# A new written-out issue order for a fused S4 convolution and Hedgehog attention kernel

## The chip, the cores and the metric

The kernel runs on one core of one Trainium2 chip. The metric is device time in microseconds (us), the median of several runs. Shorter is better.

## The reference

For tokens u of shape 1 x 2048 x 512 the kernel computes a gated mix of two branches:

```python
g = sigmoid((u * gate_w).sum(-1, keepdims=True))
# branch a: S4 convolution, one kernel of length 2048 per channel
K = real(einsum("dn,dnl,dn->dl", C, exp(dt * A * l), dt * B))   # 512 channels, 128 states
a = irfft(rfft(pad(u)) * rfft(pad(K)))[:2048] + u * Dskip
# branch b: linear attention, 32 heads of 16, with a learned feature map
q, k, v = split(u @ wqkv)                      # both branches read u
phi(t) = concat(softmax(t @ w_phi), softmax(-(t @ w_phi)))
o = (phi(q) @ (phi(k).T @ v)) / (phi(q) @ phi(k).sum(0) + 1e-6)
b = o @ wo
return g * a + (1 - g) * b
```

## The kernel before, in words

The kernel is not written as loops that run in order. Five builder functions (`prepare`, `keys_and_spectrum`, `attention_keys`, `plan_queries`, `plan_conv`) add 1046 nodes to a `Plan`. A node is one step on one engine: a group of matmuls on TensorE (PE), one or a few instructions on VectorE (DVE) or ScalarE (ACT), or the issue of DMAs from SyncE (SP). Nodes are created unit by unit, but `Plan.run` calls them in the order that the string `ORDER` gives: two characters for each node, a number in base 64. Each engine runs its own instructions strictly in the order in which they were issued, and the framework adds the semaphores that the data needs. So `ORDER` decides what stands in front of what in each of the four queues. Four more strings go with it:

- `SIDES`: for each node that may run on either of two engines, which one. These are mostly the copies out of PSUM (ACT or DVE), and some output DMAs (SP or ACT).
- `RINGS`: for each PSUM tile that may lie in either of two rings (`ps`, and `p0` early or `pf` late; two buffers each), which one.
- `FOURS`: for each of 16 units of 32 channels, whether the two partial products of the tile `A` are added on DVE (`A3`, line 1077) ahead of 64 matmuls, or left apart, with 128 matmuls.
- `ZPS`: for each of 8 pairs of token tiles, whether PE sums the exponentials of the keys in groups of four (`zp`, line 697) ahead of a short DVE reduction (line 706), or DVE reduces them alone (two instructions, line 703).

A node is named here by its kind and its number in the order of creation. What the names mean, in the order of the stages:

- Start: `par`, `wtr`, `xtr`, `ud`, `wv`, `wsm`, `ld` load parameters and tokens (`wtr` and `xtr` transpose on the way). `tg1`, `tgs`, `tga` build Fourier tables. `st1` to `st3`, `pzw` and `pzr` split the state matrix and carry it through DRAM. `psri`, `p_t`, `p_d`, `p_px` and others starting with `p_` build polar tables. `wps` and `wpe` fold `w_phi` into the weights, and `at1` lays `w_phi` out for that.
- Keys: `pk` (PE), `ek` (ACT, two exponentials), `zk` (DVE), `rz` (ACT), `vp` (PE), `vb` (a copy), `vr` (DVE), `kn` (PE). `gps` is the gate's product.
- Spectrum of u, between the keys: `udc`, `psAu`, `XAu`, `psBu`, `XU`, and `xuw`, which stores the tile `xst` to DRAM as `XUd`. `xst` has two buffers.
- Kernel generation for 16 units: `argC` and `cs` (sines), `argE`, `E` and `El` (exponentials), `A1`, `A2`, `A3`, `Rh`, `Rl` (DVE products), `kps` (PE), `KD` (a copy). ACT switches its table between sines and exponentials (`tabT`, `tabL`).
- Transforms for quarters of the channels: `psA`, `XA`, `psB`, `XK`, `t128`, `t64` or `t32` (DVE), `psz`, `Zr`; `zw` stores Z to DRAM, `zr` reads it back turned; `psy` (PE) and `ou` (DVE, with the gate). The last unit goes through `pszn`, `Zn` and `psyn` without DRAM.
- Queries: `pq`, `eq`, `zs`, `z1` to `z5`, `aw`, `ar`, `em`, `ops`, `oT`, `pya` or `bps`, `bs3`, `bsg`. Names that end in L belong to the last of the four blocks of queries. `out` and `outL` store the result.

SP issues all loads and nearly all stores, in one queue.

Of the kernel before, what the change touches and what calls it, by code (L numbers as in the profile page):

```python
# [70 lines left out]
class Plan:  # L71

    DIGITS = "0123456789abcdefghijklmnopqrstuvwxyzABCDEFGHIJKLMNOPQRSTUVWXYZ-_"
    ORDER = ("0B0C000a0H0K012K0L0j0k0I0J0l2E0D0g0d0y0M0P0_0S2F0z070U0V042H0T052I2B112J2x0E0A2z0s0p0q140m12020W0Y0N0X0n0v2y0b0e0h0i0O0Z"
             "100Q0616080f0t1d13150u2C192L2M171a1b0-"
             "1c0R1n1o1p1e1y1H031q1w0c181f1g1I2G091x1S1z1A1J1r1R1O1B0F0G2R2S1s2T2U1E1C1Q2N1K2P2D2Q2O4r1F1Y4q4x4z4E4F4y4A4M4N4B4C4I4J1M"
             "1N4D4K4G4O4T4P0r0w0x4X1Z4U4Q4R4S4Y4H4L4s4_51504V4W522v56571P4Z0o2V5a53544-2W5b555e5f2X1h582Y5c5g5l5h2Z2_5p1D2-"
             "3159305d5i5j335m5q5k325t5v5u5w1i1G34355n5r37381T365A5o5s5x5B393b1j3c5y5E5I5F5K5z1t3a3d3f5C5G5P5J3F3e3k5D3g3h3m5L3l3n1U5T"
             "5M5N3r5H5Q5O2w3t3u6a6c1u1V5U5R3G5V3o3s3H3I4t5S3y5W5X6b3A3B6d5Z3z3C6e1W5Y5-3J1L3K6f6g5_60613L3N3v3M3O3P3Q3w2A1X1-"
             "3R3T27201_213p223i3S1k283V1l3U292d622a233W3X3Y3Z2b2e3-"  # L80
             "243_1m402c2f252o2g2h4144453x46472q262i4b3D482p4d2j4c2k496h2l3E4e4i2r4k4l2s4a2m2t2n421v4f4v4j3j2u8a4m4n3q4w6i89636j646667"
             "43688e6l8d65694g4o8b6m6n8f4h4p888c6k6o8k8l6p6t718h8g8_6q8m8q8i906u8j8n8o6v6w6x8r8w8N6y6z6A8p8s8x8t6B8u8O6C728E6D6E8F737A"
             "7B758v8y746F927C8K768G6G6H8z8L777D8A8C8P6I6r78798B8H8I8Tab8J8U8Dac6J7a7ba27E7F91a38M7c8Q7G7H7d9U7e8R9Y9Z8S8V8W6K6L6M6N6P"
             "6Qa49V9-6O6T6Vad6Ra56Sa87f9Xa07g7Ia9a69W9_7h7i6s6Ua18X8Y93ahapaq7J7j8Za76X6Zaiar7K8-ay9baz7k7l6-"
             "7L7M7maa9caebL7N6YbPaf986W9d7q7r7n7o7pavag7sbQajakaA949j9kaw7u7ObMbR9l7v7P7Qasat7w9eaE9f9r9z95969sbOau7R9A7SbT7T7U9galam"
             "aF6_anaoax7xbNaB7Z7t7ybS7-"
             "bUbVbWaPaCaD97aG9t7VaMaN7zaH999aaQ9B9m9n4uaO7W7X9oaI7YaKaSaJaL7_bY9u80bX81bZ9v9wb_aYaZ8384c09CaR9Dc2c38270aT8586a-"
             "aU879EaVa_b0b1aW9x9ycgchb-"
             "9p9qc1c4c8c9c5b49hc6bcb5b6bdcicmc7cnbe9i9F9GdMdNdOdPcp9HcacbbkbldQdRb7b8cqcDcjckdScGb2dTcldUdV9I9J9N9O9P9KcvaXbfbgb9cc9L"
             "9McecrcfdW9QcocHbmcwcscdctezeAbh9RcE9SeIeJeBdCcudDdXdYdG9TdIeKdHcxcybabncFczcJdZcBcAcCeCeDeFe1e2eGbocPcQcRd-"  # L90
             "cXd3dFcYeEeHd4cIbpeOcZcSc-endKbbeoepd_e0e3dbeLcTdEcKcMcUc_d0e4d1cVcLdJbqdLbibjbrb3bsdcbtbyePeMeNfRcNd5fSd2bueQeRcOddbvd6"
             "d7bwd8fXdedffoeSetbzfrfsbAfpfubxeUeVfqe5fvfTdgeubBeTbCbDd9e6evdhcWeWeqerf2f3esdpeXftfwfxdidaeYf4eZfyfYfUfVbEfzdjdkdldqdm"
             "dndre-fWf5f6fAdsfBewe_exf7f8f0fCdodte7f9bIeyfDf1fZfafdfefffEduf-f_dvg0fbg1fFfce9fGg2e8eddzeefHg3g4g5eaebg6fgbJfIg7g8dwfh"
             "g9gagbfJfMfNbFfifKbGgcecfOefegeheiejfLflgdgebKgffPfQekfjdAelfmfndxdyggfkghdBemgjgkglgibH")
# [532 lines left out]
def attention_keys(P, nc, g, psum, r):  # L627
# [40 lines left out]
    for s2 in range(8):  # L668
# [20 lines left out]

        def ps4(K=K, box=box, on=P.ZPS[s2] == "1"):  # L690
            if not on:
                return
            box.ps = bank("zk")
            for u in range(2):
                e = K.E[:, u].rearrange("p g (h a b) -> p (g h) a b", a=4, b=4)
                for k in range(4):
                    nc.tensor.matmul(box.ps[:, 256 * u:256 * u + 256], lhsT=g.ident[:], rhs=e[:, :, k, :], start=(k == 0), stop=(k == 3), skip_group_check=True)

        def rd(K=K, box=box, on=P.ZPS[s2] == "1"):
            K.Z = g.kwk.tile([128, 2, 2, 32], F32, name="Zk")  # L700
            if not on:
                for u in range(2):
                    nc.vector.tensor_reduce(out=K.Z[:, u].rearrange("p g h -> p (g h)"), in_=K.E[:, u].rearrange("p g (h f) -> p (g h) f", f=16),
                                            axis=mybir.AxisListType.X, op=ALU.add)
                return
            nc.vector.tensor_reduce(out=K.Z[:].rearrange("p u g h -> p (u g h)"), in_=box.ps[:].rearrange("p (z b) -> p z b", b=4), axis=mybir.AxisListType.X, op=ALU.add)
            box.ps = None
# [318 lines left out]

def plan_conv(P, nc, g, psum, r):
# [566 lines left out]
```

## Time and profile before

| what | value |
|---|---|
| median of 3 runs | 261.48 us (260.12 to 264.59) |
| span of the profiled execution | 263.8 us, 9862 instructions |
| busy: PE | 199.3 us, 76% |
| busy: DVE | 225.5 us, 85%, 306 instructions |
| busy: ACT | 215.2 us, 82%, 300 instructions |
| busy: POOL | 10.2 us, 4% |
| DMA | 38.0 MB, mean 144 GB/s |

The span is the time from the first to the last instruction of the profiled execution; the page gives no other time for it, so this is taken as its own time. It lies 2.3 us above the median of the runs. More than three quarters of the chain that ended last lies on DVE (37%), PE (20%) and ACT (20%): no one engine holds it all along, and the stages must be read one by one.

### The profile page before, as it was taken

How to read it: one execution, taken by the hardware profiler on the slowest of the kernel's cores; microseconds unless marked ns; L12 is line 12 of the kernel's file. 1: busy time of each engine (PE TensorE's matmuls, PEld its weight loads, DVE VectorE, ACT ScalarE, POOL GpSimd, SP SyncE). 2: the span in 40 equal slices, each digit the busy share in tenths (PEclk: the TensorE clock that was granted, in tenths of full speed). 3: DMA queues.
4: the chain of work that ended last, by engine and by line, in shares of the span. 5: the costliest groups of instructions: out<-in, count | busy, mean ns of one | idle time of the engine just before them, and what ended most of it. 6: DMA issues, size and time to landing. Idle time of an engine off the chain costs nothing.

```text
span 263.8 us, 9862 instructions
## 1 busy us (share of the span) xinstructions
PE 199.3 (76%) x4394; PEld 137.6 (52%) x4416; DVE 225.5 (85%) x306; ACT 215.2 (82%) x300; POOL 10.2 (4%) x22
## 2 busy tenths in 40 slices
PE   0028999999856557898776869789997699989850
PEld 0018445755544323464454648555875667965640
DVE  5579396998799999999999998999999999996330
ACT  4947489995999998999999998999969999573230
POOL 4018000000000000000000000000000000000000
PEclk9999999999997799999886897999999999999995
DMA  7989991006181683602317154267656369897676
GB/s 172 148 165 232 183 204 39 4 2 210 34 252 29 192 244 93 194 4 80 107 53 187 46 187 142 82 202 200 195 150 210 102 211 233 244 227 145 128 132 102
DMA packets 79627, 38.01 MB, mean 144 GB/s; under 512 B 58593, under 2 KB 74593, under 8 KB 79585
## 3 DMA queue, kind: packets, MB, share of 16 engines
q1 hardware_dynamic: 77440, 36.66, 55.2%
q10 hardware_dynamic: 2144, 0.72, 1.3%
q8 instruction: 34, 0.56, 1.0%
q14 instruction: 9, 0.07, 0.1%
HBM read 21.12 MB, written 13.11 MB: 130 GB/s over the span
## 4 chain that ended last, share of the span: by engine, by line
DVE 37%; PE 20%; ACT 20%; issue 9%; DMA 9%; SPq 1%; POOL 1%; ACTq 0%; DVEq 0%; POOLq 0%
DVE R L1088 4%; DVE A L1072 4%; PE pk L676 4%; DVE R L1084 3%; PE vp L724 3%; DVE A L1067 3%; DVE E L1020 2%; DVE t L1198 2%; DMA XUd<-xst 2%; ACT L65 2%; DMA ZT<-Zd 2%; ACT Ek L68 2%; ACT cs L68 2%; DVE Eq L880 2%; ACT XK L147 2%
## 5 line engine op out<-in xcount | busy, mean ns | idle before, releaser
L68 ACT ACTIVATE cs<-args 128x1024 bf16<-128x1024 f32 x32 | 30.9, 1068 | 0.8 <-PE args L990 0.8
L181 PE MATMUL kps<-R,A 128*32 128x64 bf16 x1536 | 28.6, 232 | 2.7 <-DVE A L1072 1.4
L181 PEld LDWEIGHTS <-A 128*32 128x32 bf16 x1536 | 26.4, 161 | 7.0 <-DVE A L1072 2.0
L1067 DVE TENSOR_TENSOR A<-Ctab,Dtab 128x2048 bf16<-128x2048 bf16 x16 | 19.5, 1220 | 0.7 <-PE kps L181 0.7
L68 ACT ACTIVATE Ek<-pk 128x512 bf16<-128x512 f32 x32 | 16.8, 604 | 3.8 <-PE pk L676 3.8
L1088 DVE TENSOR_TENSOR R<-E,cs 128x2048 bf16<-128x2048 bf16 x16 | 19.5, 1221 | 0.1
L1084 DVE TENSOR_TENSOR R<-E,cs 128x2048 bf16<-128x2048 bf16 x16 | 19.5, 1221 | 0.0
L1072 DVE TENSOR_TENSOR A<-Ctab,Dtab 128x2048 bf16<-128x2048 bf16 x16 | 19.5, 1220 | 0.0
L147 ACT CAST XK<-psB 128x1024 bf16<-128x1024 f32 (+1 forms) x17 | 16.2, 994 | 2.4 <-PE psB L194 2.0
L68 ACT ACTIVATE E<-args 128x1024 bf16<-128x1024 f32 x16 | 16.9, 1060 | 1.0 <-PE args L1012 1.0
L724 PE MATMUL vp<-WW,xT 128*128 128x512 bf16 x59 | 16.7, 411 | 1.1 <-issue 0.9
L1198 DVE TENSOR_TENSOR t<-XUX,XK 128x2048 bf16<-128x2048 bf16 x14 | 16.9, 1222 | 0.2 <-ACT XK L147 0.2
L68 ACT ACTIVATE Eq<-pq 128x512 bf16<-128x512 f32 (+1 forms) x28 | 16.7, 696 | 0.2 <-PE pq L810 0.2
L676 PE MATMUL pk<-WW,xT 128*128 128x512 bf16 x58 | 16.2, 410 | 0.7 <-issue 0.5
L147 ACT CAST XA<-psA 128x1024 bf16<-128x1024 f32 (+1 forms) x15 | 14.6, 1015 | 2.5 <-PE psA L188 2.4
L147 ACT CAST Zr<-psz 128x1024 bf16<-128x1024 f32 x15 | 15.4, 1043 | 0.9 <-ACT Zr L147 0.6
L810 PE MATMUL pq<-xT,Wqp 128*128 128x512 bf16 x64 | 15.3, 380 | 0.6 <-ACT Eq L68 0.6
L1230 PE MATMUL psz<-t,TI 128*128 128x512 bf16 x49 | 14.6, 381 | 0.9 <-ACT E L68 0.3
L583 PE MATMUL psB<-XAu,TB 64*128 64x128 bf16 x256 | 10.3, 226 | 6.2 <-ACT xst L147 4.8
L147 ACT CAST xst<-psB 128x1024 bf16<-128x1024 f32 x12 | 11.8, 1040 | 2.8 <-DMA XUd<-xst 2.7
L65 ACT ACT_TABLE_LOAD x10 | 12.8, 1283 | 0.9 <-PEq L1578 0.7
L194 PE MATMUL psB<-XA,TB 128*128 128x128 bf16 (+2 forms) x192 | 10.3, 204 | 4.0 <-ACT XA L147 2.2
(201 smaller groups left out, 477.3 us busy)
## 6 DMA issues: line engine op xcount, KB each, us to landing
XUX<-XUd SPq DMA_DIRECT2D x32, 256.0 KB
XUd<-xst SPq DMA_DIRECT2D x8, 512.0 KB
ax<-apd SPq DMA_DIRECT2D x16, 256.0 KB
Zd<-Zr SPq DMA_DIRECT2D x15, 256.0 KB
ZT<-Zd SPq DMA_DIRECT2D x12, 256.0 KB
UD<-in_A_u_dram SPq DMA_DIRECT2D x16, 128.0 KB
XUd<-xst SPq DMA_DIRECT2D x8, 256.0 KB
out_dram<-xT SPq DMA_DIRECT2D x6, 96.0 KB
```

Of the source, the lines that this page charges most:

```text
L65: return self.nc.scalar.preload_act_table_set(name)
L68: return self.nc.scalar.activation(**kw)
L147: self.nc.scalar.copy(out=o, in_=i)
L181: nc.tensor.matmul(kps[32 * dj:32 * dj + 32, g4, e, :], lhsT=A[:, ka, :, :, d].rearrange("p a b -> p (a b)"), rhs=R[:, kr, d, :], start=(i ...
L676: nc.tensor.matmul(box.ps[:], lhsT=xT[:, st, kt, :], rhs=g.WW[:, kt, :], start=(kt == 0), stop=(kt == 3))
L724: nc.tensor.matmul(box.ps[:], lhsT=xT[:, st, kt, :], rhs=g.WW[:, 4 + kt, :], start=(kt == 0), stop=(kt == 3))
L810: nc.tensor.matmul(box.ps[:, m - m0, :] if late else box.ps[:], lhsT=g.Wqp[:, kt, 128 * m:128 * m + 128], rhs=xT[:, 4 * b:4 * b + 4, kt, : ...
L1067: nc.vector.tensor_tensor(out=c.A[:, 0:2].rearrange("p o a b c -> p (o a) b c"), in0=g.C[U // 8][:, 0:2, :, d0 % 256:d0 % 256 + 32].rearra ...
L1072: nc.vector.tensor_tensor(out=c.A[:, 2:4].rearrange("p o a b c -> p (o a) b c"), in0=g.C[U // 8][:, 1:3, :, d0 % 256:d0 % 256 + 32].rearra ...
L1084: nc.vector.tensor_tensor(out=c.R[:, :, :, 32:64], in0=t.E[:, 1].unsqueeze(1).to_broadcast([128, 2, 32, 32]), in1=t.cs[:], op=ALU.mult)
L1088: nc.vector.tensor_tensor(out=c.R[:, :, :, 0:32], in0=t.E[:, 0].unsqueeze(1).to_broadcast([128, 2, 32, 32]), in1=t.cs[:, ::-1, :, ::-1], o ...
L1198: nc.vector.tensor_tensor(out=box.t, in0=Ls[r0 // ns].X[:], in1=box.XK[:].unsqueeze(1).to_broadcast([128, 2, 1024]), op=ALU.mult)
```

## The change

The five strings are replaced; nothing else. The operations are the same but for what `FOURS` and `ZPS` select. The diff, with the long strings cut:

```diff
-    ORDER = ("0B0C000a0H0K012K0L0j0k0I0J0l2E0D0g0d0y0M0P0_0S2F0z070U0V042H0T052I2B112J2x0E0A2z0s0p0q140m12020W0Y0N0X0n0v2y0b0e0h0i0O0Z"
...
+    ORDER = ("0H0I0J0L0g0h0i190K0M2x0S0y0z0A0W2y000T0P0X0N0U0405060_0708090B0C0D110Y0V0j0k0l2R1216100O0102030d0e0f132B2C2D2N0Z140-0Q17"
...
-    SIDES = ("111110001100000110100100101100000111010000000000111111000011010100000001000010000001000000000100000000000000001000100000"
-             "00000000011000000100000000000000101000101")
+    SIDES = ("101100000000001001000101110101001100000000000000001011101110111111000001110010000001000000000100010000000000001000000000"
+             "00000100001111110000000000000010000011100")
-    RINGS = ("11010000000000000000000000000000000000000000001001000000000000101110110100011101001101110111001001011111110000000")
+    RINGS = ("00111100000000000000000000101000000000000000100100011010000000111100111110100110010111001111110011110100001001011")
...
-    FOURS = ("0101010101011100")
-    ZPS = ("01100011")
+    WARM = ("0")
+    FOURS = ("0111111111111100")
+    ZPS = ("00000110")
```

`WARM`, which asks for matmuls that only keep PE busy, is all zeros before and after.

Read node by node, `SIDES` moves 46 nodes: 26 from ACT to DVE, 17 from DVE to ACT, `at1` from POOL to DVE, and the output DMAs `out#7` and `outL#1` from ACT to SP. To DVE go, among others, three `oT`, all four `bsg`, both `Zn`, `XK#16`, `Zr#14` and `KD#3`; to ACT go six `XAu`, four `vb` (with `vb#0` and `vb#1`), `KD#5`, `KD#9`, `XA#16` and `oTL#1`. `RINGS` moves 43 tiles. `FOURS` adds units 2, 4, 6, 8 and 10 to those without `A3`. `ZPS` turns the PE sum off for pairs 1, 2 and 7 and on for pair 5.

The order itself is read best as the four queues. The first work on the keys, before and after:

```text
PE  before  psri#2 psri#0 psri#1 wps#2 wps#3 wps#0 wps#1 gps#0 pk#0 pk#1 vp#0 pk#2 zp#0 vp#1 pk#3
PE  after   wps#2 wps#0 psri#0 psri#2 wps#3 psri#1 wps#1 pk#0 pk#1 pk#2 pk#3 vp#0 zp#0 zp#1 vp#1 gps#0
DVE before  dt2 w1 st1#1 st2#1 st3#1 st1#0 st2#0 st3#0 p_t#8 p_t#0 p_t#1 p_t#9 p_t#2 p_t#5 p_t#3 wpe#0 p_t#6 p_fc#0 vb#0 zk#0 vb#1
DVE after   w1 dt2 st1#1 st2#1 st1#0 st3#1 p_t#8 p_t#0 p_t#1 st2#0 st3#0 p_t#3 p_t#9 p_t#5 p_t#2 p_t#6 p_fc#0 p_t#4 p_t#7 zk#0 zk#1 vr#0
ACT before  dtc p_e p_g p_d#7 p_d#4 wpe#2 wpe#3 p_d#6 p_d#0 wpe#1 ek#0 ek#1 ek#2 p_d#2 p_d#3 rz#0
ACT after   dtc wpe#2 p_e wpe#3 wpe#0 p_g p_d#7 p_d#2 wpe#1 p_d#0 p_d#3 ek#0 ek#1 ek#2 ek#3 p_d#1 rz#0 vb#0 vb#1
SP  before  wtr par#3 par#0 xtr#3 ld xtr#1 par#5 par#4 wsm par#2 par#1 xtr#2 xtr#0 wv ud#2 ud#1 ud#0 ud#3 pzw#1
SP  after   par#5 wsm par#1 par#2 wtr ld par#0 par#4 xtr#0 par#3 xtr#2 xtr#3 xtr#1 pzw#1 wv ud#0 ud#1 ud#2 ud#3
```

And the last stage:

```text
PE  before  psz#10 psz#11 argE#14 psA#12 psy128#2 psA#13 opsL#0 pya#3 psy128#3 psB64#0 psB64#1 pya#4 kps#14 psz#12 psA#14 psy128#4
            psz#13 psB32#0 pya#5 psy128#5 opsL#1 kps#15 psz#14 psA#15 bpsL#0 bpsL#1 psB32#1 psy64 pszn#0 pszn#1 psyn#0 psyn#1 psy32
PE  after   psz#10 psA#12 psz#11 psA#13 pya#3 psy128#3 argE#15 psB64#0 opsL#0 psB64#1 opsL#1 kps#14 psz#12 psA#14 psz#13 pya#4
            psy128#4 psB32#0 pya#5 psy128#5 kps#15 psz#14 psA#15 bpsL#0 bpsL#1 psB32#1 psy64 pszn#0 pszn#1 psyn#0 psyn#1 psy32
DVE before  t128#11 Rh#15 A1#14 A2#14 ou#2 Rh#14 El#14 Rl#14 El#15 ou#3 A3#14 t64#0 t64#1 Rl#15 A1#15 A2#15 ou#4 A3#15 t32#0 t32#1
            ou#5 KD#9 XA#16 oTL#1 bs3#3 t32#2 t32#3 ou#6 Zn#1 ou#8 ou#9 ou#7
DVE after   t128#11 A1#14 Rh#14 El#14 A2#14 ou#3 Rl#14 A3#14 t64#0 t64#1 Rh#15 El#15 A1#15 Rl#15 A2#15 A3#15 t32#0 t32#1
            ou#5 Y#2 Zr#14 ou#4 bs3#3 bsg#0 bsg#1 bs3#4 bsg#2 bsg#3 t32#2 XK#16 t32#3 ou#6 Zn#0 Zn#1 ou#9 ou#8 ou#7
ACT before  tabL#4 XK#11 E#15 KD#6 Zr#10 Zr#11 E#14 XA#13 XA#12 oTL#0 XK#13 XK#12 KD#7 Y#1 XA#14 Zr#12 Zr#13 XK#14 out#1 KD#8
            Y#2 XA#15 Zr#14 bs3#4 XK#15 XK#16 bsg#0 Zn#0 bsg#1 bsg#2 bsg#3 outL#1 out#7
ACT after   tabL#4 KD#6 E#14 Zr#10 Zr#11 XA#12 XA#13 E#15 XK#12 Y#1 XK#13 oTL#0 KD#7 Zr#12 XA#14 Zr#13 oTL#1 XK#14 out#1 KD#8
            KD#9 XA#15 XA#16 XK#15
SP  before  zw#10 xup#14 zw#11 xup#13 zr#4 zr#5 xup#15 zw#12 zw#13 zr#6 zr#7 zw#14 out#3 out#2 zr#8 zr#9 out#0 out#4 outL#0 out#5 out#6
SP  after   zw#10 zw#11 out#0 zr#4 xup#14 zr#5 zw#12 zw#13 zr#6 zr#7 zw#14 out#3 out#2 outL#1 zr#8 zr#9 outL#0 out#4 out#5 out#6 out#7
```

More of the change, by code (lines that the diff above doesn't have):

```diff
@@ L73 @@
     DIGITS = "0123456789abcdefghijklmnopqrstuvwxyzABCDEFGHIJKLMNOPQRSTUVWXYZ-_"
-    ORDER = ("0B0C000a0H0K012K0L0j0k0I0J0l2E0D0g0d0y0M0P0_0S2F0z070U0V042H0T052I2B112J2x0E0A2z0s0p0q140m12020W0Y0N0X0n0v2y0b0e0h0i0O0Z"
[L75 to L94, printed above, removed]
@@ L95 @@
-    SIDES = ("111110001100000110100100101100000111010000000000111111000011010100000001000010000001000000000100000000000000001000100000"
-             "00000000011000000100000000000000101000101")
-    RINGS = ("11010000000000000000000000000000000000000000001001000000000000101110110100011101001101110111001001011111110000000")
-    WARM = ("000000000000000000000000000000000000000000000000000000000000000000000000000000000000000000000000000000000000000000000000"
-            "000000000000000000000")
@@ L100 @@
-    FOURS = ("0101010101011100")
-    ZPS = ("01100011")
+    ORDER = ("0H0I0J0L0g0h0i190K0M2x0S0y0z0A0W2y000T0P0X0N0U0405060_0708090B0C0D110Y0V0j0k0l2R1216100O0102030d0e0f132B2C2D2N0Z140-0Q17"
+             "151a1b2S0R1w1c1n1H0a0b0c1o1e1d1p1y2H2I2J1I2T2U1z1x2A1A2K2L2M1f1g2E2F2G2O1S1C1J1E1R182P1M1B2Q1F1q1r1s0E0F0G0m0n0o4q1K4x4z"
+             "1N4y4A4M1Y4N4O4E4B0p0q0r1D1G4P4Q4C4R1L4D4F0s0t0u4I4G4J4r4T0v0w0x4K1Z4X4U2V1O4H4s4S4Y2W1T4L4_4V514t2X564Z4W502Y4-521U2Z5e"
+             "532-5a572_54315b1V325f5g5558305c5h5l333459355d5t1P375i5m365j385u5v5k5p5q2v5n395A1h1i1j3b5r5w5o3a5B5s5I3c5x5y5K3d3f5J3F5E"
+             "3g3e5z5C5P5F5L3k3m5M5Q5G3G5D1Q1k1l1m3l3h3i3j5T5H6a5N5O5U6c3H3r3n5R5V5S3o3p3q5W6b6d3I6e1W5X3s5Z3t5Y5-6f3y3u5_3z3A3J606g3B"
+             "1t1u1v611X623K3v3w3x3L3N1-1_3O3P3M2763203R21286h3Q293S2264232b3T3V2d2a3U243W3X3Y3Z3_2f3C3D3E6i252h2c2e403-44462o2j66652g"
+             "456j414243474b2q2i6l2p2l2k262s48494a2w4c4d2r4i4e2m4f4g4h4j2n2t4k2u6m8a674l4m4n4o4v4w89686n4p698e8b6k8d8f6o886p6u8c6w8g8h"
+             "8k8q6t8l8i6y8m8n8j8o6x6v8r6z8w8s716A8p6B8N738O726C8t8x6D8u758E6E8F8G6q6r6s766F8v778P6G8K8y8H788T8I6H7A8L6I6J6K7C748z796L"
+             "6M6N7B8A7a8J8B7b8U6O8C7E8Dab7G7D8M929394ac8Q6P6Q6R7ca27Fa37H7d6T8R6V8_90918S6Sad9U8V7e9Y6X6W6U7f7g7h9Z8W9X6Ya5a87i7j7k8X"
+             "a08Ya49V9-a68Za97Iah9W7lai8-a7aa7q9_a1ayaz7sae7Jap4u6Zaq9b7m7n7oaf7K7r7t7Lag7paj7M9c6-7N7u9jakaMaNaO7O7P7QarbL9d9k7vaEav"
+             "2z9l7w9eas7R7S7T7xbP7U9f6_9rbQ9z9saw9A959697alanat7V7W7X7Z9g9h9iaA7YamaobMaF7_au98999abRaxbO8070bT817-7yaB82aC9t83bN7zaD"
+             "9B84aPaQaRaGbSaHbVbUbYbW85aI869mb_87bXaK9uaJ9nbZc2aSaTaUc0aLcpc39o9p9qc49vaY9Cb4aZcqb-c1c8a-c99w9x9ybcb5cgc59DcGcHcI9E9F"
+             "9Gchb6dMbdc6cicrdNc7dOcmcaaVaWaXdPbecnbkcba_bldQb09H9I9J9K9L9Mcvb7ccb1b2b3dRcjcddSckb8dT9NdUcecfbfbm9OcldVeIeJcwcJcKcLb9"
+             "babbbgcodWdXdYcDcEcFez9PdCbhbibj9QcscteA9RdGdHcueKbnbocxcydZd-d_9SeB9TeFeCdDczdIe1e2e3e0e4cBdEbycCcAdJcPcXeDeGdFeEeOcQcY"
+             "cRdKeHbpbqbrcScZd3bsbtbubvbwbxcTbzd4eLePc-cMcNcOeMdbewexeyd5cUcVcWc_dceNd0d1d2bAeQfoeneoepdddLd6eRfreSfpdeeUd7dfeTeqeres"
+             "bBbCfueVfqd8d9dafRfseWbDe5fvfSeXf2fte7dgdhdibEbFbGbHf3eYe6djdkdlfwf4eZfXfTfxfye-f5fUfzf6e8eteuevfYdpdmdndodqfAfVdsfWdte_"
+             "f0f1f7f8f9fBbIbJbKfCfZfafbfcfDf-f_dudvfEg0e9fdfeffg1fFdreafGfHfIg2dzdAdBedebeceeefdwdxdyg3egg4g6g5g7fgg8ekelemfJfKfLg9fh"
+             "gagbfMfNfOgceheiejgegffifjfkgdflfmfnfPfQggghgigjgkgl")
```

## The prediction

> **What bounds the kernel now.** I read five views: the slices of the page, the table of busy time by stretch, the waits, the groups by line, and the chain that ended last. Instructions carry the names of the plan, numbered from 0 (`zk#1` is the second key sum).
>
> The slices say where to look:
>
> ```profile
> PE   0028999999856557898776869789997699989850
> ...
> DVE  5579396998799999999999998999999999996330
> ACT  4947489995999998999999998999969999573230
> ...
> PEclk9999999999997799999886897999999999999995
> ```
>
> VectorE (DVE) and ScalarE (ACT) are both full from about 30 to 217 us; each is open before 33 us and after 240. The table by stretch gives the idle time (columns: stretch, length, busy time of each engine, clock, DMA share, GB/s):
>
> ```profile
> 0.00:30.00 30.00, 10.68 (x126) 8.55 (x128) 19.45 (x52) 18.67 (x27) 10.19 (x22) 1.00 0.97 181
> 30.00:60.00 30.00, 29.58 (x435) 16.89 (x436) 24.95 (x35) 26.62 (x50) 0.00 (x0) 1.00 0.36 72
> 60.00:75.00 15.00, 12.36 (x264) 8.53 (x260) 11.96 (x16) 12.16 (x25) 0.00 (x0) 1.00 0.51 151
> ...
> 130.00:150.00 20.00, 15.01 (x412) 11.07 (x414) 19.96 (x23) 19.90 (x26) 0.00 (x0) 0.74 0.31 88
> ...
> 217.00:240.00 23.00, 21.88 (x613) 17.64 (x618) 22.05 (x24) 16.02 (x20) 0.00 (x0) 1.00 0.92 226
> 240.00:264.00 24.00, 12.66 (x466) 8.54 (x464) 7.19 (x11) 5.84 (x11) 0.00 (x0) 0.85 0.67 118
> ```
>
> DVE idles 10.6 us before 30, 8.1 from 30 to 75, 3.1 from 75 to 240 (span by span, 165 us less busy time) and 16.8 after. So a new order can gain at the start, between 30 and 75, and at the end; between 75 and 240 it must take work off DVE and ACT together, since both are full. The waits name the three places:
>
> ```profile
> DVE vb L149 <- PE vp L724: 6.4, 3, 4.5
> ...
> DVE t L1201 <- ACT XK L147: 3.5, 1, 3.5
> ...
> ACT xst L147 <- DMA XUd<-xst: 2.7, 1, 2.7
> ```
>
> The sum is made against the profiled execution: span 263.8 us, which is 2.3 above the median of 261.48 and inside the runs' 260.12 to 264.59. I carry the difference over to the median.
>
> **The start: -2.5 us.** Before, TensorE (PE) runs the gate product `gps` (1.9 us) ahead of `pk#0`, and DVE's first key work is `vb#0`, which waits 4.5 us for `vp#0`; `zk#0` starts at 32.67. Now `pk#0` to `pk#3` come first, `gps` later, and `vb#0`, `vb#1` are read by ACT. The last token transpose is issued behind the same other loads, so xT lands as before, at 24.5 (the last count of its semaphore in the trace). The second gate is DVE's polar products, which free PSUM: from `dt2` at 15.9, four instructions of the split (0.6, 0.35, 0.6, 0.6 apart), eight products at 0.6, `st2#0` 0.35 and `st3#0` 1.4 end with `p_t#6` near 24.7, against 26.8. The third, ACT's four copies `wpe`, ends near 22.4 (15.6 + 4 x 1.0 + 0.6 + 1.1 + 2 x 0.55). So `pk#0` starts at 24.8, not 27.3: -2.5. Four matmuls cost 1.7 there (0.42 each in this row, 0.26 later) and `ek` 1.2, so `zk#0` starts between 28 and 30. Bounds: 0 (something else gates) to -4. `at1` moves from POOL to DVE; its nearest DVE row, a 128x1024 product, is 0.69, POOL took 1.50, and it lies under ACT's sines (DVE waits 4.0 us for those). It costs nothing; without that cover, 0.7.
>
> **30 to 75 us: -1.5.** Here PE is 29.58 of 30 busy. ZPS takes the PE pre-sum (1.08) off pairs 1, 2 and 7 and gives one to pair 5: PE -2.2, DVE 3 x 1.74 - 1.74 = +3.5 (L703 below, twice 1.21, against one L706). The 2.7 us of ACT and 1.0 of DVE at 66 are reads of `psB` into `xst`, which has two buffers; the first store takes 5.4 us. Before, 5.4 us of DVE work stands between `XU#1` and `XU#4`; now 7.8 (four at 0.6, `zk#5` now 0.6 to 0.7 by its row if PE is in time, copies, and reads): at least the ACT wait should shrink. `psAu#0` now comes earlier and needs all of UD, which lands about 1.3 us later behind `pzw#1`: 0 to +1 us. Bounds for the stretch: -4 to +2; I take -1.5, nearer to nothing, as the order is tight in new places.
>
> **75 to 240 us: -2.7.** Group rows:
>
> ```profile
> L1077 DVE TENSOR_TENSOR A<-A 128x2048 bf16<-128x2048 bf16 x8 | 9.8, 1220 | 0.0
> ...
> L703 DVE TENSOR_REDUCE Zk<-Ek 128x64 f32<-128x1024 bf16 x8 | 9.4, 1213 | 0.0
> ...
> L706 DVE TENSOR_REDUCE Zk<-zk 128x128 f32<-128x512 f32 x4 | 2.7, 686 | 0.8 <-PE zk L697 0.8
> ```
>
> FOURS drops `A3` (L1077) for units 2, 4, 6, 8, 10: 5 x 1.22 = -6.1 on DVE; each such `kps` has 128 matmuls, not 64: 2.35 against 1.22, 5 x 1.13 = +5.7 on PE, which has room in 108:190 and little after. Up to `A3#15` the reads that leave DVE sum to 14.1 us and `ou#4` (1.22) is put later; those that come, with `at1`, sum to 15.0. With ZPS: -6.1 + 3.5 - 14.1 - 1.2 + 15.0 = -2.9 on DVE. By running sums up to `t128#11` it is -0.8, and -1.3 with the 0.09 us that each of five more back-to-back instructions overlaps. ACT up to the table load `tabL#4` has the same work (-0.3); `E#15` (1.0) now stands behind `Zr#11`.
>
> What this does to the last chain is seen at its head:
>
> ```profile
> 222.94 4.64 DMA Zd<-Zr
> 228.06 4.91 DMA ZT<-Zd
> ...
> 242.44 1.14 DVE oT L149
> 243.63 1.04 PE bps L913 x4
> ```
>
> `Zr#11` goes to DRAM, comes back (9.6 us), and `psy128#4` waits for it; then `pya#5`, `psy128#5`, `opsL#1`, `kps#15` (ends 239.4). Walked with the rows' durations from `t128#11`, taken at 214.1 (219.4 less 4.0 from above and 1.3 of work): `Zr#11` 216.9, `zr#4` 222.3 (5.4 later, as before), `psy128#4` not before 226.7. PE itself reaches it at 227.8 (`kps#14` ends 222.9, then `psz#12`, `psA#14`, `psz#13`, `pya#4`: 1.0, 0.64, 1.0, 2.4). Then 0.63, 0.95, 1.5, 0.63 and `kps#15` 1.21: 232.7. That is 6.7 before 239.4, 4.0 of it from the first two terms: -2.7 is left. Bounds: -0.3 (ACT's saving alone) to -4.6 (DVE's with `kps#15` no longer behind `opsL#1`). In SP's queue `out#0` now stands between `zw#11` and `zr#4` and waits for `ou#3`, at 219.3 in this walk, so it has 3 us to spare; if that cover is gone, each us of `ou#3` is one of `zr#4`. `xup#14` ahead of `zr#5` waits for `t64#0` (222.7) and adds 0.9, covered by `pya#5`.
>
> **The end: -1.1.** Before, `bpsL#1` waits for `oT` on DVE (row above) and `psB32#1` starts at 245.64 behind it; now ACT reads `oT` early: -0.2. All `bsg` and `XK#16` are on DVE in line with `t32#2`, `t32#3`: +0.5. `outL#1` (on SP now, behind `bsg#3`) stands ahead of `zr#8`, `zr#9`: they land up to 1.6 later, `psy32#0` +1.1 at most. After the last product at 257.2 SP still issued this:
>
> ```profile
> 257.13 1.96 SPq L962 DMA_DIRECT2D out_dram<-xT  x2
> 259.13 2.11 SPq L1348 DMA_DIRECT2D out_dram<-xT  x4
> ```
>
> 4.1 us; now only `out#6`, `out#7` are left, four issues, 2.0 us: -2.1. Between -0.9 and -1.5; -1.1. The Trainium skill (DMA: Bandwidth & Descriptors, section Issuing engines are not separate DMA queues) says that issuing from a second engine saves only that engine's issue time; by it the move of `outL#1` and `out#7` from ACT to SP costs 1.0 us each of SP time and nothing in transfer, which is the sum above.
>
> **New waits: +1.5.** A written-out order runs each queue strictly; a late instruction holds all behind it. DVE idles 3.1 us in 75:240 of the order before. I allow half of that; bounds 0 to 8 (the 8.1 of 30:75 once more).
>
> Sum: -2.5 - 1.5 - 2.7 - 1.1 + 1.5 = -6.3: span 257.5, and 261.48 - 6.3 = 255.2; I say 255.
>
> **Rivals.** (1) New waits eat the middle: the reads of PSUM moved (26 to DVE, 17 to ACT, 43 other rings) stop one of the two full queues for 5.7 us, so that only start and end are kept: -2.5 - 1.1 = -3.6, 257.9; with one more us of wait 259. For it: from 108 to 150 both are 99% busy, and no slack absorbs a miss. Against: in running sums of the rows the hand-over from ACT to DVE that is latest against its reader, `E#9` to `El#9`, lags 2.8 us less in the new lists. Chance 0.27. (2) All idle of 30:75 goes and nothing new comes: -2.5 - 4 - 2.7 - 1.5 = -10.7: 250.8. Chance 0.15. (3) Slower: PE becomes the bound from 170 on. It is 63.6 us busy of those 70 (21.88 of 23 at the end) and gets 2 x 1.13 more: 65.9 at full clock. With 4 us of earlier start and 1.5 at the end, PE may take 75.5 before all gain is lost. The granted clock halves in windows of 3.4 us (four between 130 and 161, mean 0.74 in 130:150); one such window loses 1.7 us of matmul, so it decides from six windows after 170; with ten, 65.9 + 17 - 75.5 = +7.4: 269. Against: the clock there was 1.00. Chance 0.10. The Trainium skill (TensorE: Matmul & The Clock Gate, section Part 1: The HAM clock gate) puts the half rate down to an idle window of about 3.4 us; the longest PE gap between 100 and 170 is 1.3 us, so by that rule the halved windows here should not be, and the trace disagrees. (4) The new order does not change the bound: the two full engines take as long as before: 261.5. Chance 0.08. The forecast has 0.40.
>
> **How the numbers follow.** A measurement of this kernel tells about 2% from no change: 256.25 to 266.7. Faster: the forecast's own range, 252 to 258, lies four fifths below 256.25 (0.32); with (2), 0.15, and a quarter of (1), 0.07, that is 0.54. Slower: (3), 0.10, and 0.01 of others. Same: the rest, 0.35. Range for 8 in 10: 249.5 (below (2), by its full bounds) to 262.5 (past (1) and (4)); (3) lies outside.
>
> **What would show it.** Right: `pk#0` near 25, `zk#0` before 30.5; no ACT wait on the XUd store above 1 us; `L1077` x3; DVE idle from 75 to 240 under 5 us; `kps#15` ending 232 to 236; after the last DVE product at most four output DMAs on SP. Wrong: `psy128#4` waiting for ZT behind `out#0`; a PSUM read on DVE or ACT that starts over 1 us late with PE waiting for its buffer; a clock under 0.9 from 170 to 240; `udc#3` waiting for UD.

## The result, and the profile after

| | median | range, runs | ratio to before, 95% interval |
|---|---|---|---|
| before | 262.42 us | 260.12 to 264.59, 4 | |
| after | 270.21 us | 269.06 to 271.32, 4 | 1.0323 [1.0249, 1.0397] |

The new order is 3.2% slower, about 8.5 us (7.8 by the two medians), where 6.3 us of gain was forecast. The profiled execution of after took 269.06 us with a span of 267.0: 2.1 lie around the span. The forecast took the span of before, 263.8, as that execution's own time. A second profile of the same kernel (below) took 263.75 us with a span of 262.0, so the first ran near 265.6, above all four timed runs. The sum compares stages, so it does not move by this, but start stages read from that profile may be late (see the second look below).

Ratios below are to the kernel before on the same chip. They leave out runs more than 1.5% above the fastest of their kernel; where the median of all runs says something else, both are given. A ratio is turned into us with 262.

The slices and the table by stretch of after (the same columns as for before, with 75 to 240 in one row) come first; the last row is before over the same 165 us:

```profile
PE   0241999999855858899758868789998687999760
...
DVE  7687598999999988997799978999989599799841
ACT  6966499998999999999887997899879968884000
...
PEclk9996599999995797999788999999999999999995
```

```profile
0.00:30.00 30.00, 8.65 (x63) 6.24 (x65) 21.03 (x55) 21.10 (x29) 9.81 (x21) 0.87 0.91 167
30.00:60.00 30.00, 29.63 (x493) 17.51 (x498) 26.57 (x35) 27.07 (x52) 0.00 (x0) 0.96 0.50 88
60.00:75.00 15.00, 13.52 (x257) 8.67 (x254) 14.24 (x20) 13.42 (x24) 0.00 (x0) 1.00 0.64 178
75.00:240.00 165.00, 134.34 (x3278) 94.03 (x3289) 151.41 (x184) 148.87 (x183) 0.00 (x0) 0.94 0.52 147
```

```profile
75.00:240.00 165.00, 133.98 (x3117) 95.11 (x3129) 161.91 (x195) 151.91 (x191) 0.00 (x0) 0.94 0.53 154
```

Up to 75 us DVE now idles 13.2 us (75 less the busy times) where it idled 18.6. From 75 to 240 it idles 13.6 where it idled 3.1. The full rows of nines of DVE and ACT now have sevens and eights in them. The waits and the groups by line say for what:

```profile
DVE Eq L876 <- DMA ax<-apd: 8.4, 6, 2.3
...
PE pk L672 <- DMA xT<-in_A_u_dram: 5.6, 1, 5.6
```

```profile
L876 DVE TENSOR_TENSOR Eq<-Eq,ax 128x2048 bf16<-128x2048 bf16 x8 | 9.8, 1223 | 8.4 <-DMA ax<-apd 8.4
...
L1073 DVE TENSOR_TENSOR A<-A 128x2048 bf16<-128x2048 bf16 x3 | 3.7, 1223 | 0.1
```

L1073 is `A3` (L1077 before), now three times, as forecast. L876 is `em`, the product of the queries' exponentials with their normalising factor. The factor takes a way through DRAM: `aw` stores it (64 KB), `ar` reads it back spread over all partitions into the tile `ax` (two halves of 512 KB, two DMAs each), `em` multiplies. In the profile of before no row of the waits names `ax`. Now six of the eight `em` wait for it, and the chain that ended last runs through it three times:

```profile
123.18 8.76 DMA ax<-apd
...
155.47 8.37 DMA ax<-apd
...
204.05 6.71 DMA ax<-apd
```

These are 8.9% of the span; the read of `ax` had no share in the chain of before. Why the read came late is seen in SP's issues (start, length, what), after first, then before:

```profile
120.09 1.39 SPq L869 DMA_DIRECT2D ax<-apd  x2
121.58 0.91 SPq L1147 DMA_DIRECT2D XUX<-XUd  x2
122.54 1.24 SPq L869 DMA_DIRECT2D ax<-apd  x2
123.82 1.80 SPq L1147 DMA_DIRECT2D XUX<-XUd  x2
```

```profile
121.41 2.65 SPq L873 DMA_DIRECT2D ax<-apd  x4
```

The new order puts `xup#1`, a read of 512 KB, between the two halves `ar#0` and `ar#1`, and `xup#0` right behind them. In the order before, `xup#0` and `xup#1` went out at 102.8 and 106.8. At the same time `em#0` and `em#1` moved forward. Before, they ran at 130.9 and 133.9, 9.5 and 11.0 us after their read was issued, and waited for nothing. Now DVE is ready for them 5.3 and 8.5 us after it, and they start 1.8 and 1.0 us later, at 127.2 and 132.0, when the data have landed. Before first, then after:

```profile
130.93 1.22 DVE L880 TENSOR_TENSOR Eq<-Eq,ax 128x2048 bf16<-128x2048 bf16 x1
...
133.87 1.22 DVE L880 TENSOR_TENSOR Eq<-Eq,ax 128x2048 bf16<-128x2048 bf16 x1
```

```profile
127.16 1.23 DVE L876 TENSOR_TENSOR Eq<-Eq,ax 128x2048 bf16<-128x2048 bf16 x1 [1.77 <-DMA ax<-apd]
...
132.04 1.23 DVE L876 TENSOR_TENSOR Eq<-Eq,ax 128x2048 bf16<-128x2048 bf16 x1 [1.04 <-DMA ax<-apd]
```

### The profile page after: what moved, and what is told of

Same layout as the page of the kernel before. It is cut to its first block, busy times and chain, and to the rows that moved or that the text cites. A ratio compares the mean times of both kernels' runs of the same rounds, so it can differ in the third digit from the quotient of the medians.

```text
span 267.0 us, 10472 instructions
## 1 busy us (share of the span) xinstructions
PE 203.2 (76%) x4699; PEld 138.9 (52%) x4720; DVE 228.7 (86%) x313; ACT 213.8 (80%) x292; POOL 9.8 (4%) x21
## 4 chain that ended last, share of the span: by engine, by line
PE 40%; DVE 18%; DMA 13%; ACT 12%; SPq 10%; issue 5%; DVEq 0%; ACTq 0%
DMA ax<-apd 9%; PE kps L177 6%; PE pk L672 6%; PE vp L720 4%; SPq L492 4%; ACT cs L68 3%; PE pq L806 3%; PE psz L1226 3%; PE psy L787 2%; DMA xT<-in_A_u_dram 2%; ACT E L68 2%; SPq L869 2%; SPq L1466 2%; PE psB L190 2%; ACT xst L143 1%
## 5 line engine op out<-in xcount | busy, mean ns | idle before, releaser
L177 PE MATMUL kps<-R,A 128*32 128x64 bf16 x1856 | 33.4, 229 | 3.0 <-DVE R L1084 1.6
L177 PEld LDWEIGHTS <-A 128*32 128x32 bf16 x1856 | 31.3, 161 | 8.0 <-DVE R L1084 2.5
L672 PE MATMUL pk<-WW,xT 128*128 128x512 bf16 x58 | 17.4, 432 | 6.2 <-DMA xT<-in_A_u_dram 5.6
L806 PE MATMUL pq<-xT,Wqp 128*128 128x512 bf16 x64 | 17.2, 408 | 1.6 <-ACT Eq L68 1.6
L143 ACT CAST Zr<-psz 128x1024 bf16<-128x1024 f32 x14 | 14.3, 1020 | 4.3 <-issue 3.8
L876 DVE TENSOR_TENSOR Eq<-Eq,ax 128x2048 bf16<-128x2048 bf16 x8 | 9.8, 1223 | 8.4 <-DMA ax<-apd 8.4
L720 PE MATMUL vp<-WW,xT 128*128 128x512 bf16 x59 | 15.9, 392 | 0.7 <-issue 0.5
L699 DVE TENSOR_REDUCE Zk<-Ek 128x64 f32<-128x1024 bf16 x12 | 14.1, 1211 | 2.4 <-ACT Ek L68 2.4
L184 PE MATMUL psA<-W,KD 128*64 128x128 bf16 x256 | 10.4, 227 | 4.4 <-DVE XA L145 1.3
L579 PE MATMUL psB<-XAu,TB 64*128 64x128 bf16 x256 | 10.9, 240 | 3.8 <-ACT xst L143 2.5
## 6 DMA issues: line engine op xcount, KB each, us to landing
UD<-in_A_u_dram SPq DMA_DIRECT2D x16, 128.0 KB, 4.7
```

The lines of the kernel that those rows point to most:

```text
L143: self.nc.scalar.copy(out=o, in_=i)
L177: nc.tensor.matmul(kps[32 * dj:32 * dj + 32, g4, e, :], lhsT=A[:, ka, :, :, d].rearrange("p a b -> p (a b)"), rhs=R[:, kr, d, :], start=(i ...
L672: nc.tensor.matmul(box.ps[:], lhsT=xT[:, st, kt, :], rhs=g.WW[:, kt, :], start=(kt == 0), stop=(kt == 3))
L720: nc.tensor.matmul(box.ps[:], lhsT=xT[:, st, kt, :], rhs=g.WW[:, 4 + kt, :], start=(kt == 0), stop=(kt == 3))
L806: nc.tensor.matmul(box.ps[:, m - m0, :] if late else box.ps[:], lhsT=g.Wqp[:, kt, 128 * m:128 * m + 128], rhs=xT[:, 4 * b:4 * b + 4, kt, : ...
```

## The experiments

**Which part of the order loses.** After 412 nodes both orders have done the same nodes but for one, after 966 but for four. So each can be divided there and joined to the other, with the engines, rings and forms of each part.

```diff
 s_start      new[:412]  + old rest
 s_end        old[:966]  + new rest
 s_mid        old[:412]  + new up to node 966 + old rest
 s_start_end  new[:412]  + old up to node 966 + new rest
```

> First third new, the rest old: the first 412 of the 1046 nodes in the new order with the new engines, rings and ZPS, then all others in the old order with the old engines, rings and FOURS (the two orders have the same nodes behind them there but for one). Reading of the profiles: the new order reaches kvbd 3 to 4 us earlier (102.8 and 101.5 against 105.7), so the time falls by 3 to 4 us to 258 to 259. Rival: the old rest hangs on something else of the start (the landing of a load, the table of sines) and the gain is under 1 us.

> The last 80 nodes new, all before them old: the end from about 240 us in the new order with its engines and rings. Reading of the profiles: from the end of psy128#5 to the end of the span the new order takes 24.0 to 24.2 us, the old one 25.8, so the time falls by 1 to 2 us to 260 to 261. Rival: the end of the new kernel is short only because its stores were already out, and here nothing is gained.

> Only the middle new: nodes 413 to 966 in the new order with its engines, rings and FOURS, start and end old. Reading of the profiles: from kvbd to psy128#5 the new order takes 140.0 us, the old one 130.5, so the time rises by 8 to 10 us to 270 to 272. Rival: the middle loses only because the new start hands it its work in another state; then it rises by less than 4 us.

> Start and end new, the middle old. If the parts add up, 5 to 6 us under the kernel before, 256 to 257.5. If the old middle takes the gain of the start back, 260 to 262.

| | ratio | us against before | forecast for the part |
|---|---|---|---|
| s_start | 1.0020 [0.9982, 1.0058] | +0.5 (-0.5 to +1.5) | -4.0 |
| s_mid | 1.0357 [1.0296, 1.0417] | +9.3 (+7.7 to +10.9) | -1.2 (work -2.7, new waits +1.5) |
| s_end | 1.0047 [1.0009, 1.0086] | +1.2 (+0.2 to +2.2) | -1.1 |
| s_start_end | 0.9990 [0.9959, 1.0021] | -0.3 (-1.1 to +0.5) | -5.1 |

The middle carries the loss. Start and end bring no gain, against what was expected of them; the end alone even loses 1.2 us, which does not show in the combination with the new start. s_mid has the same wait as the new order:

```profile
DVE Eq L877 <- DMA ax<-apd: 8.0, 6, 2.2
```

**A second look at before** (the kernel is unchanged).

> The kernel before, unchanged, for a second profile. In the first one zk#0 ends at 35.0 us, in two kernels with the same issue order but other FOURS or ZPS at 33.1 and 33.4. If the first profile started late by chance, zk#0 ends at 33 to 33.5 here, the span is 259 to 261 and the later milestones are 2 us earlier; the forecast's start term then set the new order against a late one. If not, zk#0 is at 35 again.

Time 263.75, span 262.0, `zk#0` ending at 34.5: late again, not 33. Over the kernels with the old start `zk#0` ends at 33.0 to 35.0, over those with the new start at 31.0 to 32.9. So the new start does lead in the profiles, by about 2 us, but the profiled executions of before lay above the median of its runs, and s_start's time does not show the lead.

**Taking the wait away.** The product takes the tile itself as second factor, which leaves the normalising factor out of the result; the read is still issued.

```diff
-nc.vector.tensor_tensor(out=e, in0=e, in1=Q.ax[:, 2 * ip:2 * ip + 2], op=ALU.mult)
+nc.vector.tensor_tensor(out=e, in0=e, in1=e, op=ALU.mult)
```

> The new order with the products em taking the tile itself as second factor in place of ax, so that they do not wait for the broadcast read; the read is still issued and moved, the product costs the same. It leaves the normalising factor of the queries out of the result. If those waits (8.4 us on DVE in the new order) cost path time, the time falls by 5 to 8 us, to 262 to 265. If PE holds the middle (through the 128 matmuls of kps or the order of ops in its queue), DVE idles elsewhere and the time falls by less than 2 us, to 268 to 270.

> The kernel before with the same cut as v7_no_ax: em takes the tile itself as second factor, the broadcast read is still issued (the normalising factor is left out of the result). In the old order no em waits for the read, so the time stays within 1 us of 261.5; then the 6 to 7 us of v7_no_ax are those of the waits. If the cut itself saves (a product without a second tile, a buffer freed earlier), it falls here by 3 us or more too.

In the new order: 1.0028 [0.9969, 1.0088] (median of all runs 264.26, 1.9 us above that of before). In the old: 1.0011 [0.9957, 1.0064]. Leaving the factor out saves nothing by itself, and takes 7.7 us (1.0323 less 1.0028) off the new order, or 5.9 by the medians of all runs. The profiles price it lower still: from the end of `kps#0` to the end of `kps#15` after takes 132.9 us, v7_no_ax 128.0 (4.9 less) and the second profile of before 127.2. Another 1.9 us between after and v7_no_ax stand ahead of `kps#0`, in a stretch that both kernels share. So the wait for `ax` is most of the loss, 5 to 8 of the 8.5 us.

**Moving the products later.** The eight `em`, with `ops` and all behind them, 4 to 8 DVE nodes later (`em#0` behind `A2#3`, `em#1` behind `Rh#4`, and so on).

> The new order with the eight products em (queries' factor times the broadcast tile ax) and what hangs on them moved 4 to 8 DVE nodes later, so that each stands behind work that does not need the broadcast read; all else as in the new order. H1 (DVE waits for the broadcast read of the factor at em#0, em#1, em#4, em#5 and emL#0, emL#1, 8.4 us, are on the path): those waits fall under 1.5 us, DVE idle from 75 to 240 us falls from 13.6 to 6 or 7, and the time falls by 6 to 8 us against the new order, to 262 to 264. Rival H2 (ACT and PE are as late as DVE, so that the waits only stand where others would): the idle time reappears behind PE or ACT and the time stays at 269 to 271.

1.0555 [1.0479, 1.0631], 276.34 us: six slower than the new order, where H1 wanted 6 to 8 faster. No `em` waits for `ax`, but PE, which takes its own queue in order, now stands in front of `ops`:

```profile
PE ops L895 <- DVE Eq L876: 13.2, 6, 3.6
...
DVE A L1063 <- PE kps L177: 7.9, 5, 3.0
```

The wait was only handed to PE, and from there to the next `A1` on DVE, which needs the buffer that `kps` reads. The experiment moved too much and could not decide between H1 and H2.

> The new order with its own operations, in which three short stretches are put in another order: each em stands 1 to 3 DVE nodes later, behind products that have their data, as late as its factor lands in the trace of the new order (em#0 after A1#3, em#1 after oT#0, em#4 after A2#6, em#5 after A1#7, emL#0 after A2#12, emL#1 after Rh#13); what reads it on PE stands later too (ops#8, ops#9 behind kps#6, ops#2 behind em#1), so that PE is not held as in v1_em_late; ar#1 and ar#5 go ahead of the reads xup#1 and xup#2 on SP; psy128#2 goes behind kps#13. If the 8.4 us of waits for ax make the loss, DVE waits for ax under 2 us in all and the time falls by 5 to 8 us to 262 to 265, with a right result. If only taking the factor away helps, it stays above 267.

The four runs of this reordering lie between 265.15 and 273.25, median 270.36, and no ratio is given for them. In the profiled one no `em` waits for `ax`, but in the second stretch DVE waits for other things and `kps#7` ends at 171.9, as late as in the new order (171.4). The median lies where the forecast put it if only leaving the factor out helps. But work on PE was moved too, so the run does not decide it; like v1_em_late it shows that starting `em` later need not pay.

**Moving the reads on SP alone.**

```diff
 v13  SP  aw#0 ar#0 -xup#1 ar#1 +xup#1 xup#0 ... ar#4 -xup#2 ar#5 +xup#2
 v15  SP  +xup#1 +xup#0 aw#0 ar#0 -xup#1 ar#1 -xup#0 ... ar#4 -xup#2 ar#5 +xup#2
 v14  as v15, and DVE  A1#12 -emL#0 -emL#1 A2#12 +emL#0 Rl#12 Rh#13 +emL#1
```

> The new order with two moves on SP only: ar#1 ahead of xup#1 and ar#5 ahead of xup#2. In the new order the 512 KB read xup#1 is issued between the halves ar#0 and ar#1, and DMA runs at 220 to 254 GB/s from 124 to 130 us; in the old order xup#0 and xup#1 were issued at 103 to 107, long before. If the shared bandwidth delays the factor, em#1 and em#5 start 1 to 3 us earlier and the time falls by 1 to 3 us. If the delay is that of the broadcast read itself (arL#1 lands 3.5 us after arL#0 with nothing between), the time stays within 0.7 us of 270.2.

> The new order with three moves on SP only: xup#0 and xup#1 ahead of aw#0, where the old order has them (they were issued between and behind ar#0 and ar#1), and ar#5 ahead of xup#2. If shared DMA bandwidth delays the factor, em#0 and em#1 now wait under 1 us together (2.8 in the new order), and the time falls to 265 to 267, as far as or a little further than with ar#1 moved ahead of xup#1 (266.9). If the read's own time is the cause, no more than there: 267.

> The same three moves on SP, and emL#0 behind A2#12, emL#1 behind Rh#13 (nothing on PE reads them before 231 us). DVE's waits for ax come to under 2 us in all, kps#12 ends 3 to 4 us earlier against kps#11 and the time falls by another 2 to 3 us, to 263 to 265, with the factor kept: what is left against the kernel before is then the rest of the middle. If PE or ACT holds the stretch from 203 to 217 us, the time stays at that of the kernel with the SP moves alone.

| | ratio | median of all runs | DVE's wait for ax in the profile |
|---|---|---|---|
| new order | 1.0323 [1.0249, 1.0397] | 270.21 | 8.4, 6 times |
| v13_ar_first | 1.0150 [1.0085, 1.0215] | 266.91 | 5.9, 5 times |
| v15_xup_early | 1.0112 [1.0060, 1.0164] | 264.62 | 3.8, 3 times |
| v14_xup_em | 1.0056 [1.0011, 1.0100] | 265.32 | 0.8, 2 times |

Three issues moved on SP, and nothing else, give back 5.5 of the 8.5 us (3 to 8 by the two intervals), with the factor kept. v13_ar_first, which moves only `ar#1` and `ar#5`, already gains more than the 1 to 3 us expected of it; the intervals of the two overlap. In v15 the first pair runs at 123.2 and 126.9, 5.3 and 7.6 us after its read is issued, and waits for nothing; what is left of the waits is at `emL#0` and `emL#1` (3.6), where no XUX read stands between. By the median of all its runs v14 gains nothing over v15 (265.32 against 264.62), so its further gain is not settled. Its profiled run took 266.28, and shows a wait in the start that the forecast had listed as a danger:

```profile
DVE UDp L145 <- DMA UD<-in_A_u_dram: 3.2, 2, 3.0
```

How the read itself uses DMA is seen where nothing else is issued. The first row is before, behind `ar#0` and `ar#1`; the second is after, with `xup#1` and `xup#0` beside them; the third is v15 (last columns: DMA share, GB/s):

```profile
124.00:126.00 2.00, 1.48 (x16) 0.53 (x17) 2.00 (x3) 1.97 (x4) 0.00 (x0) 1.00 0.51 184
```

```profile
124.00:126.00 2.00, 2.00 (x125) 1.96 (x128) 1.40 (x2) 2.00 (x5) 0.00 (x0) 1.00 0.81 254
```

```profile
122.00:124.00 2.00, 2.00 (x128) 2.00 (x128) 2.00 (x3) 2.00 (x5) 0.00 (x0) 1.00 0.55 188
```

Alone the read keeps about half of the 16 DMA engines busy and moves 184 to 188 GB/s; at that rate its 1 MB takes 5.7 us. With the XUX reads beside it the total is 254, but `ax` comes later: its second half lands 11.9 us after `ar#0` is issued (132.0 less 120.1), in v15 no later than 9.0 (126.9 less 117.9). Of these 2.9 us SP's issue of `xup#1` explains 0.9.

The Trainium skill (DMA: Bandwidth & Descriptors, section Rules for kernel authors) says that a DMA uses no more engines than the outermost dimension of its access patterns has room for, and names a broadcast as the example. The source of `ar` has 8 outermost, and the share of 0.51 agrees with 8 of 16. By that rule a pattern with 16 outermost would halve the 5.7 us; this is an estimate, and was not tried.

**The operations, each alone.** `FOURS` and `ZPS` of the new kernel in the old order, and the old ones in the new order (the old `ZPS` but for pair 2):

```diff
 v3_fours     old order   -FOURS 0101010101011100  +FOURS 0111111111111100
 v4_zps       old order   -ZPS 01100011            +ZPS 00000110
 v8_oldfours  new order   -FOURS 0111111111111100  +FOURS 0101010101011100
 v9_oldops    new order   the same, and -ZPS 00000110 +ZPS 01000011
```

> The kernel before, in its own issue order, with the new FOURS only: units 2, 4, 6, 8 and 10 without the DVE addition A3 (5 x 1.22 = 6.1 us off DVE) and with 64 matmuls more each (5 x 1.13 = 5.7 us onto PE). If DVE holds the middle, as the prediction's term of -6.1 has it, the time falls by 3 to 6 us to 256 to 259. If PE or ACT holds it as much as DVE, it stays within 1 us of 262, or rises by up to 3 where the added matmuls stand behind 190 us, where PE has little room.

> The kernel before, in its own issue order, with the new ZPS only: the PE pre-sum of the keys' exponentials off for pairs 1, 2 and 7 and on for pair 5: DVE +3.5 us, PE -2.2 us. If DVE is on the path between 30 and 75 us, the time rises by 2 to 3.5 us to 264 to 266. If PE is (29.6 us busy of the 30 from 30 to 60), it falls by 1 to 2 us to 260 to 261. If the stage has slack on both, it stays within 1 us.

> The new order with the old FOURS: A3 on DVE again in units 2, 4, 6, 8 and 10 (+6.1 us of DVE) and 64 matmuls fewer in each (-5.7 us of PE). If the added matmuls cost here what they cost in the old order (+6.9), the time falls by 4 to 7 us, to 263 to 266. If the DVE time taken off was used by this order, whose sequence was made for it, the time rises by 3 to 6 us, to 273 to 276; if the tile A's single buffer makes the two forms equally long (A3 and 64 matmuls 2.44, 128 matmuls 2.35), it stays within 1.5 us of 270.

> The new order with the old FOURS and with ZPS 01000011, which is the old one but for pair 2 (its PE pre-sum finds no PSUM buffer in this order). Almost the old operations in the new order. If FOURS and ZPS make the loss (+6.9 and +5.0 in the old order) and the order is as good, it comes to 260 to 264. If the order itself makes it (the waits for the broadcast read), it stays at 268 to 273.

| | ratio to before | reading |
|---|---|---|
| v3_fours | 1.0216 [1.0104, 1.0327] | FOURS costs 5.7 us in the old order (6.9 by the medians of all runs) |
| v4_zps | 1.0154 [1.0084, 1.0224] | ZPS costs 4.0 us in the old order (5.0 by the medians) |
| v8_oldfours | 1.0514 [1.0439, 1.0588] | the old FOURS costs 5.0 us in the new order |
| v9_oldops | 1.0681 [1.0618, 1.0744] | with the old ZPS too, 9.4 us |

Neither form is better as such. v3_fours and v4_zps rise by more than was expected of them, and v9_oldops, near 280 us, lies above both of its forecasts. ZPS in the old order costs about the 3.5 us that it puts on DVE, which fits DVE being on the path of the keys. FOURS takes 6.1 us off DVE there, and the time still rises. The rows from 108 to 240 us of before and of v3, and v3's waits on DVE in that stretch:

```profile
108.00:240.00 132.00, 112.93 (x2788) 83.25 (x2799) 129.85 (x139) 119.72 (x156) 0.00 (x0) 0.95 0.52 151
```

```profile
108.00:240.00 132.00, 114.20 (x3059) 85.98 (x3071) 121.32 (x129) 117.01 (x150) 0.00 (x0) 0.96 0.50 145
```

```profile
DVE A L1067 <- PE kps L181: 4.5, 5, 1.3
DVE t L1198 <- ACT XK L147: 2.0, 3, 1.4
```

DVE idles 10.7 us where it idled 2.2. The tile `A` has one buffer (capacity 1 in the plan). Without `A3`, `kps` holds it 2.35 instead of 1.22 us, and the next `A1` waits for it unless other DVE work stands between. This wait grew by 3.8 us (0.7 before); most of the other new idle time stands behind ACT. In the new order, with more units of this form, the same wait is 0.9 us in all. So an order made for one form seems to have that other work in place, and an order made for the other not; this is argued from the waits and was not tested by itself.

**Smaller tries.** The loads in another issue order, and two stores moved in a version with the new start:

```diff
 v5_loads        SP  wtr par#5 wsm xtr#0 par#1 par#2 ld xtr#2 par#0 par#4 xtr#3 par#3 xtr#1
 v10_start_tail  s_start, and SP  zw#12 +out#0 zw#13 ... zr#8 zr#9 -out#0 +outL#0 out#4 -outL#0 out#5 out#6
```

> The new order with only the issue order of the loads changed on SP: wtr par#5 wsm xtr#0 par#1 par#2 ld xtr#2 par#0 par#4 xtr#3 par#3 xtr#1, the two transposing loads first. If the order in which the loads are issued decides when the last transposed tokens land (26.8 us in the new order), they land at 24 to 25, pk#0 starts 2 us earlier and the time falls by 1 to 2 us. If the transposes take the queue's time wherever they stand, they land at 26 to 27 and the time stays within 0.5 us of the new order's 270.2.

> A try at a version under both: the new start (412 nodes) and the old rest, with two output stores moved on SP in the old end: out#0 ahead of zw#13, where SP is idle, and outL#0 ahead of out#4, so that only out#4's second half, out#5 and out#6 are left after the last product. In s_end the shorter queue of stores was paid by psy32 waiting for Z; here the reads of Z stay ahead of the stores. Expected: 1 to 2 us under s_start's 261.6, 259.5 to 260.5. If the transfers' own time ends the kernel, not their issue, no gain: 261 to 262.

v5_loads: 1.0258 [1.0176, 1.0341], 269.34 us, overlapping the new order's interval. In its profile `pk` no longer waits for xT, but `p_t#6` on DVE, the second gate, ends at 27.6 instead of 24.2, and `pk#0` ends at 28.4, inside the 27.2 to 29.3 seen with this start. v10_start_tail: 0.9992 [0.9950, 1.0033]: no gain. No version tried here beats the kernel before.

## Why the prediction was wrong

**What held.** The operation counts and durations: `A3` three times, at 1.22 us. No wait of ACT on the XUd store. `zk#0` starts at 30.0, before the 30.5 named as a sign. DVE's idle time up to 75 us fell by 5.5, but this is no time gained: the stretch also holds the 3.5 us of DVE work that ZPS adds. Two stores, four issues, 1.9 us after the last product, as said. The clock from 170 to 240 stayed at 1.00, so rival (3), PE as the bound through halved windows, did not come. `xT` landed at 27.0 in this profile, not 24.5, as the second transpose held SP for 5.0 us; in others with the same start `pk#0` ended up to 2 us earlier.

**What failed: "New waits: +1.5".** It was not worked out from the new queues but taken as half of the old idle time. DVE's idle time from 75 to 240 rose by 10.5 instead. 5 to 8 us of time hang on one wait, that of `em` for `ax` (v7_no_ax, with v12_before_no_ax beside it), and about 5.5 on where three reads stand on SP (v15_xup_early). The prediction followed SP's queue at the tail (`out#0` before `zr#4`, `xup#14` before `zr#5`, `outL#1` before `zr#8`), but not for the queries: `aw`, `ar`, `em` and the `xup` between them are not in it. The trace of before had all that was needed. `em` ran 9.5 to 11.0 us after the issue of its read there, and the new order is ready for it after 5.3 and 8.5, with 1 MB more in flight.

**The second failed step: "75 to 240 us: -2.7".** It let DVE's saving pass on to the chain, with PE's 5.7 us free of charge in 108 to 190. In v7_no_ax, with no wait for `ax`, the time is that of before. From the end of `kps#0` to the end of `kps#15` DVE has 4.1 us less work there than in the second profile of before (121.3 against 125.5), idles 5.0 us more (6.7 against 1.7), and so takes 128.0 us instead of 127.2. `kps#15`, forecast to end between 232 and 236, ends at 237.2 (at 244.0 in the new order). From 108 on the waits name ACT and PE at ten instructions, none above 1.8 us:

```profile
DVE t L1194 <- ACT XK L143: 2.3, 2, 1.8
DVE A L1063 <- PE kps L177: 1.3, 2, 0.9
DVE R L1080 <- ACT E L68: 0.9, 1, 0.9
```

That these are one cause is not shown; v3_fours shows one of them, the buffer of `A`. A second candidate is SP's queue again. In the chain that ended last of v7_no_ax a store of Z goes out at 213.8 us behind four XUX reads, 2.9 us after its tile was written, and takes 6.2 us. That was not tested.

**The end.** The four terms of -1.1 (-0.2, +0.5, at most +1.1, -2.1) add up to -0.7 to -1.8, so its bounds of -0.9 and -1.5 were already too narrow. (The start of `psB32#1`, read as 245.64, is 245.80 in the trace; nothing hangs on it.) The -2.1 for the stores held: from the last product to the end of the span it is 4.3 us in the new order and 4.5 in s_end, against 6.6 and 6.5 in the two profiles of before. The term for `psy32` behind `zr#8`, `zr#9` was too small in s_end: from `psy128#5` to the last product it takes 20.9 us where b0_again takes 19.3, +1.6. In the new order itself this is 19.9, as in the first profile of before. These terms leave a small gain, but s_end measured +1.2, and the combination with the new start -0.3. Why the end brings nothing in the time stays open.

**The start.** -2.5 and -1.5 were read against a late execution. The lead at `zk#0` is in the profiles and not in s_start's time; whether the timed runs of before start earlier than its two profiled ones (`zk#0` at 34.5 and 35.0) stays open.

Rival (1), that new waits eat the middle, was the right kind; it looked for them at PSUM reads and priced them at 5.7 us, when they were at a transfer. The rival that ends slower was another mechanism, and the range ended at 262.5.

## What to carry to other kernels

When a hand-written order moves a consumer forward, list for every consumer of a transfer the time from the issue to the use in the old trace and in the new order, with what is issued in between on the same queue: a margin that vanishes there can cost most of its length (here 5 to 8 us of time for 8.4 us of waits), since everything behind the waiting instruction waits too. When work is taken off a full engine, ask which buffer its neighbour will now hold longer; if that is a single one, the saving can come back as a wait. Read a stage's gain against more than one profile of the kernel before.

## What the runs showed of the hardware

- The broadcast read, 8 outermost, ran at a DMA share of 0.51 to 0.55 and 180 to 194 GB/s alone (before and v15_xup_early, two windows of 2 us each), where the loads of the first 30 us of before had a share of 0.97. With nothing beside it (v15_xup_early) the first half was there within 5.3 us of its issue; that product did not wait.
- A transposing load held SP's queue 1.9 to 5.1 us for its issue in these runs, against about 0.5 for the other loads; the same `xtr#0` took 3.1 us in v5_loads and 5.0 in the new order.
- The mean granted clock was 0.949 in the second profile of before, 0.932 after and 0.903 in v9_oldops. It does not simply follow the waits: s_mid, with nearly the same waits for `ax` and the same loss as the new order, had 0.944. What lowers it was not tested.
